# Sparse attention and an MLP on one core: the weights' differences taken earlier and spread, the first two half-size products in PSUM tiles of their own, sums moved, the last store on another queue

## The chip, the cores and the metric

The kernel runs on one core of one Trainium2 chip. The core has a matrix engine (TensorE, PE in the profile; PEld is its weight load), a vector engine (VectorE, DVE), an activation engine (ScalarE, ACT), GpSimd (POOL), and SyncE (SP), which here issues DMAs alone. Each engine takes its own instructions strictly in order; semaphores tie the engines together. The metric is the device time of one execution in microseconds (us).

## The reference, cut to what matters

```python
# 4 batches, 8 heads, 768 tokens, head size 64: block-sparse attention
scores = where(mask, q @ k.T / 8, -1e9);  attn = softmax(scores)      # 24 blocks of 32 tokens
x = concat over heads of (attn @ v)                                   # 4 x 768 x 512
# then a residual MLP with affine scales
a1 = alpha1 * x + beta1
u  = x + lam * (w_tok @ a1)                # mixes the 768 tokens
a2 = alpha2 * u + beta2
out = u + lam * (relu(a2 @ w_ch1) @ w_ch2) # 512 -> 2048 -> 512
```

The mask allows a band, the first and last block, and three drawn blocks for each block of rows.

## The kernel before

The 768 tokens of a batch lie in 6 tiles of 128 partitions. Attention goes by pairs of heads, 16 in all (4 batches of 4 pairs). For one pair: scores on PE (L600) into PSUM tiles named `sp` (2 buffers of two banks) or `mm`; the exponential on ACT (L618) into `eT`; for all but the first five pairs a multiplication by a 0/1 mask on DVE (L635); the product with v on PE (L670) into the one-bank tile `op`, which has a single buffer; and on DVE the division by the row sums (L687, L688), which writes `x_sb` and sets `op` free. POOL (in a few places DVE) then makes `a1pp` from it (L704, L705). Token mixing is L844 on PE, its sum L856 on DVE, a cast `ubf` (L863), a transposition by DMA (`uraw`, L894, issued by SP) or by PE (L872), and the second affine to `uT` (L885 on DVE, L883 on ACT for the last batch). The first MLP layer is L910 on PE with a Relu on ACT (L917) into `hts`. The second layer is L930 with its sum on DVE (L939), or, for some tiles of the last two batches, the scheme below. A store of a finished tile is issued by SP (L943).

The scheme: a token tile t and the tile t+3 are taken together, and their second layer is computed with 7 half-size products in place of 8 (Winograd's form of Strassen's method). The operands are four quarters of `hts` (11, 12 for tile t; 21, 22 for tile t+3; the second digit is the half of the 2048 hidden units) and four quarters of `w2b`, the weights already scaled by lam. Needed beside them are

- the **differences** of weights, T1 to T4, 16 instructions of 128 x 512 elements in bf16 on DVE (L972), made once; they are put where the transposed q and k of the first five pairs were (`qTs`, `kTs`), and into `qk` and `tmore`;
- the **sums** S1 to S4 of hidden values for each t, 128 x 1024 in bf16 on DVE (L1018): S1 = 21 + 22, S2 = S1 - 11, S3 = 11 - 21, S4 = 12 - S2;
- the seven products (L1044), each 8 matmuls of 128 x 256, and the adds of their results to `x_sb` (L1054).

Batch 2 uses it for t = 1 and 2, batch 3 for t = 0, 1, 2. In batch 2, **product 1** of a pair goes into an `mm` tile (3 one-bank buffers, shared with the scores, both MLP layers and the token mixing). DVE adds it to the second half of tile t (128 x 256) and to both halves of tile t+3 (128 x 512). **Product 2** then accumulates onto the same bank, and the total is added to the first half of tile t (128 x 256). Since it writes to what the first two adds read, it waits for them.

The order of all work is written out by hand. After the first five pairs, the rows of `WEAVE` (`W1` 9 rows, `W2` 12, `W2L` 12, `W3` 4) list letters, and each letter emits one job on all its engines: `q` scores of three units, `x` an exponential, `k` a mask multiplication, `p` a product with v, `f` a group of the first layer, `g` the next piece of the second layer or the next product, `T` a token-mixing job, `A` the next difference, `S` the next sum of hidden values, and so on. So a letter's place in a row sets the place of its instruction in each engine's queue. `W2` runs while the pairs of batch 2 are in attention (from about 105 us on), `W2L` while those of batch 3 are (to about 234 us), and `W3` does the rest. In `W2L`, 16 `A`s stand in the first nine rows: the differences run from 172.7 to 224.9 us. Two stretches of the profile are of the same make and are spoken of below as **stretch A** (120.5 to 133 us, in batch 2) and **stretch B** (189 to 203 us, in batch 3): in both, DVE does a division, masks, two `uT` affines, masks, a division, one L939 sum, masks and a division almost without a pause.

Of the kernel before, what the change touches and what calls it, by code (L numbers as in the profile page):

```python
# [20 lines left out]
S = 768  # L21
# [21 lines left out]
W1 = [  # L43
# [9 lines left out]
]  # L53
W2 = [
# [12 lines left out]
]  # L67
W2L = [
# [12 lines left out]
]  # L81
W3 = [
# [5 lines left out]
STR = (2, 3)  # L88
HN = NH // 2
HC = DM // 2  # L90
WEAVE = W1 + W2 + W2L + W3
ENG = {
    "kT0": 0,
    "kT1": 0,
# [153 lines left out]
def kernel(  # L248
# [16 lines left out]
    nc = tc.nc  # L265
# [194 lines left out]
    def sp_tile():  # L460
        return psum.tile([P, 2, 512], FP, name="sp", tag="sp", bufs=2)
# [6 lines left out]
    def mm_tile(shape=(P, DM), dt=FP):  # L468
        return psum.tile(list(shape), dt, name="mm", tag="mm", bufs=3)

    def op_tile(shape):
        phase["op"] += 1
        if phase["first"] and phase["op"] % 2 == 0:
            return mm_tile(shape)
        return psum.tile(shape, FP, name="op", tag="op", bufs=1)
# [463 lines left out]
            nc.vector.tensor_tensor(out=x, in0=x, in1=ps[:], op=ALU.add)  # L939
            emit_store(b, o, slice(0, DM))  # L940

    def emit_store(b, o, sl):
        nc.sync.dma_start(  # L943
            out[b].rearrange("(p o) n -> p o n", o=NT)[:, o, sl], x_sbs[b][:, o, sl]
        )

# [12 lines left out]
    def b_rows(name, n, k=1):  # L959
        if name in bq:  # L960
            rows, cols = bq[name]
            return w2b[:, rows.start + n : rows.start + n + k, cols]
        m = HN * ("T1", "T2", "T4", "T3").index(name) + n
        assert m // 6 == (m + k - 1) // 6
        return tpool[m // 6][:, m % 6 : m % 6 + k]
# [3 lines left out]
    def job_t(dst, a, b, n, k=2):  # L969
        for name in (a, b):  # L970
            assert name in bq or (name, n) in did
        nc.vector.tensor_tensor(  # L972
            out=b_rows(dst, n, k),
            in0=b_rows(a, n, k),
            in1=b_rows(b, n, k),
            op=ALU.subtract,
        )
        did.add((dst, n))
# [10 lines left out]
    def a_of(b, t, name, r=slice(0, HN)):  # L989
        if name in ("X1", "X2"):  # L990
            return xs[(b, t, name)][:, r]
        c, half = {"11": (0, 0), "12": (0, 1), "21": (1, 0), "22": (1, 1)}[name]
        return hts[(b, c)][:, HN * half + r.start : HN * half + r.stop, ts(t, P)]
# [40 lines left out]
    def mul(b, t, n, ps, start, cols=slice(0, HC)):  # L1034
        a, m, need = PROD[n]
        assert m in bq or all((m, r) in did for r in range(0, HN, 2))
        if need:
            assert all(("S", b, t, need, r) in did for r in range(HN))
        c, half = {"1": (0, 0), "X": (1, 0)}.get(a[0], (1, 0))
        if need == 0:  # L1040
            h, half = divmod(int(a) - 11, 10)
            assert all(("f", b, h, HN * half + r) in did for r in range(HN))
        for r in range(HN):
            nc.tensor.matmul(  # L1044
                ps,
                a_of(b, t, a)[:, r],
                b_rows(m, r)[:, 0, cols],
                start=(start and r == 0),
                stop=(r == HN - 1),
                skip_group_check=True,  # L1050
            )

    def plus(x, ps):
        nc.vector.tensor_tensor(out=x, in0=x, in1=ps, op=ALU.add)  # L1054

    def twice(ps):
        return ps.unsqueeze(1).broadcast_to([P, 2, HC])

    lo, hi = slice(0, HC), slice(HC, DM)

    def job_p(b, t, n):
        x = x_sbs[b]
        tail = b == B - 1
        last = tail and t == NT // 2 - 1
        if n == 1 or (n == 6 and not tail):
            if n == 1 and not tail:
                banks[(b, t)] = [mm_tile()[:]]
            else:
                banks[(b, t)] = [sp_tile()[:, 0]]
        bk = banks[(b, t)]  # L1070
        if n == 7:
            bk.append(mm_tile()[:])
        elif n == (2 if tail else 3):
            bk.insert(1, mm_tile()[:])
        if n == 1:
            mul(b, t, 1, bk[0][:, lo], True)
            if tail:
                plus(x[:, t, lo], bk[0][:, lo])
            else:
                plus(x[:, t, hi], bk[0][:, lo])  # L1080
                plus(
                    x[:, t + 3].rearrange("p (h c) -> p h c", h=2), twice(bk[0][:, lo])
                )
        elif n == 2:
            ps = bk[1] if tail else bk[0]
            mul(b, t, 2, ps[:, lo], tail)
            if last or not tail:
                plus(x[:, t, lo], ps[:, lo])
            if last:
                emit_store(b, t, lo)  # L1090
        elif n == 6:
            mul(b, t, 6, bk[0][:, lo], not tail)
            plus(x[:, t + 3, lo], bk[0][:, lo])
        elif n == 7:
            mul(b, t, 7, bk[-1][:, lo], True)
            plus(x[:, t + 3, hi], bk[-1][:, lo])
        elif n == 5:
            mul(b, t, 5, bk[0][:, lo], False)
            plus(x[:, t : t + 4 : 3, hi], twice(bk[0][:, lo]))
        elif n == 4:  # L1100
            mul(b, t, 4, bk[-1][:, lo], False)
            plus(x[:, t + 3, lo], bk[-1][:, lo])
            emit_store(b, t + 3, slice(0, DM))
        elif last:
            for h in range(2):
                sl = slice(HC + h * P, HC + h * P + P)
                ps = (mm_tile(), op_tile([P, DM]))[h]
                mul(b, t, 3, ps[:, sl], True, ts(h, P))
                plus(x[:, t, sl], ps[:, sl])
                emit_store(b, t, sl)  # L1110
        else:
            mul(b, t, 3, bk[1][:, hi], not tail)
            sl = slice(0, DM) if tail else hi
            plus(x[:, t, sl], bk[1][:, sl])
            emit_store(b, t, slice(0, DM))
        did.add((b, t, n))
# [36 lines left out]
    def start_mlp(b):  # L1153
        ns = [n // 2 + HN * (n % 2) for n in range(NH)] if b == B - 1 else range(NH)
        todo["f"] += [lambda c=c, n=n: job_f1(b, c, n) for c in range(2) for n in ns]
        if b not in STR:
            todo["g"] += [
                lambda o=o, g=g: job_f2(b, o, g) for o in range(NT) for g in range(4)
            ]
            return  # L1160
        todo["g"] += [
            lambda j=j: job_p(b, *j) if len(j) == 2 else job_f2(b, *j[:2])
            for j in P_ORDER[b]
        ]
        todo["S"] += [lambda t=t, n=n, r=r: job_s(b, t, n, r) for t, n, r in S_ORDER[b]]
# [206 lines left out]
    todo["A"] = [lambda t=t, n=n: job_t(*t, n) for t in T_ORDER for n in range(0, HN, 2)]  # L1372
    for p, text in enumerate(WEAVE):
        for t in text.replace(" ", ""):
# [30 lines left out]
```

## Time and profile before

| | |
|---|---|
| median of 3 runs | 303.78 us (303.64 to 304.06) |
| profiled execution | 305.7 us, span of its instructions 304.0 us |
| busy in the span | PE 292.7, DVE 220.4, ACT 218.8, POOL 111.5 us |
| granted TensorE clock | 1.00 throughout |

The profile is of one execution. Starts are counted from the first instruction. In the timeline a row gives start, length, engine, line, operation, out<-in with shapes and xcount for successive instructions of one kind; a bracket gives the idle time of that engine before it and what ended it. Matmuls overlap each other in the records: a group of 8 with 128 x 256 is recorded 1.03 to 1.05 us long, and the next group starts 0.87 us after it began.

### The profile page before, as it was taken

Reading aid. Unit: us, or ns where it says so; the run is one execution under the profiler, and the core shown is the slowest. Engines: PE = TensorE matmul, PEld = TensorE weight load, DVE = VectorE, ACT = ScalarE, POOL = GpSimd, SP = SyncE. Lnnn points to the kernel's source line nnn. Section 1 sums busy time; section 2 is a strip of 40 time slices with the busy share of each in tenths; the row PEclk is TensorE's granted clock in tenths of the full one; section 3 lists DMA queues with packets and bytes.
Section 4 is the critical chain, followed back from the end, with each engine's and each line's share of the span. In section 5 each row is a group of like instructions: output and inputs, shape, how many; then the busy total and the mean of one; then the engine's idle time right before and its main releaser. Section 6 shows DMA issues by size and latency. Waiting matters only on the chain.

```text
span 304.0 us, 7518 instructions
## 1 busy us (share of the span) xinstructions
PE 292.7 (96%) x3113; PEld 194.1 (64%) x3113; DVE 220.4 (72%) x434; ACT 218.8 (72%) x324; POOL 111.5 (37%) x151
## 2 busy tenths in 40 slices
PE   7899999999999999999999999899998889999995
PEld 2678778665577565555675565455565667766885
DVE  4978889995688797963568897993877778204574
ACT  5999989998899954998888754898769524577100
POOL 8997877632534700564315410353322020000000
PEclk9999999999999999999999999999999999999999
DMA  6999999971491992729737592828112002200032
GB/s 178 203 195 164 189 150 198 174 124 26 94 156 40 141 188 67 133 43 152 121 56 92 104 179 75 120 64 130 44 23 54 2 32 57 112 0 2 0 115 95
DMA packets 57275, 31.09 MB, mean 102 GB/s; under 512 B 37205, under 2 KB 54017, under 8 KB 57241
## 3 DMA queue, kind: packets, MB, share of 16 engines
q0 software_dynamic: 16752, 14.22, 32.8%
q1 hardware_dynamic: 40164, 15.99, 27.3%
q8 instruction: 24, 0.39, 0.5%
q10 hardware_dynamic: 324, 0.40, 0.5%
q14 instruction: 11, 0.08, 0.1%
HBM read 29.75 MB, written 6.29 MB: 119 GB/s over the span
## 4 chain that ended last, share of the span: by engine, by line
PE 79%; DVE 9%; DMA 6%; ACT 2%; POOL 2%; issue 1%; SPq 0%; POOLq 0%
PE mm L910 25%; PE mm L930 14%; PE sp L600 8%; PE mm L844 7%; PE op L670 7%; PE mm L1044 5%; PE sp L1044 3%; DMA qpad<-in_q_dram 3%; PE mm L600 3%; DVE eT L635 2%; DMA uraw<-ubf 2%; ACT eT L618 2%; PE op L647 2%; PE mm L820 1%; DVE x_sb L1054 1%
## 5 line engine op out<-in xcount | busy, mean ns | idle before, releaser
L618 ACT ACTIVATE eT<-sp,expb 128x1024 f16<-128x1024 f32 x111 | 118.4, 1119 | 3.5 <-PE sp L600 2.9
L910 PE MATMUL mm<-uT,w1b 128*128 128x384 bf16 x512 | 91.6, 326 | 0.0
L635 DVE TENSOR_TENSOR eT<-eT,mask 128x1024 f16<-128x1024 f16 x99 | 80.8, 843 | 12.8 <-ACT eT L618 12.6
L704 POOL TENSOR_TENSOR a1pp<-x_sb,vbc 128x384 bf16<-128x384 f32 x26 | 28.7, 1105 | 131.8 <-DVE x_sb L688 96.9
L917 ACT ACTIVATE hts<-mm 128x384 bf16<-128x384 f32 x128 | 61.0, 500 | 19.3 <-PE mm L910 18.6
L910 PEld LDWEIGHTS <-w1b 128*128 128x128 bf16 x512 | 48.1, 98 | 31.8 <-issue 2.1
L618 ACT ACTIVATE eT<-mm,expb 128x512 f16<-128x512 f32 x66 | 41.7, 685 | 27.5 <-PE mm L600 27.2
L930 PE MATMUL mm<-w2b,hts 128*128 128x512 bf16 x224 | 54.7, 379 | 0.0
L670 PEld LDWEIGHTS <-eT 128*128 128x128 f16 x792 | 29.8, 98 | 10.9 <-DVE x_sb L688 2.3
L670 PE MATMUL op<-vext,eT 128*128 128x65 f16 x792 | 32.3, 194 | 1.8 <-DVE x_sb L688 0.8
L930 PEld LDWEIGHTS <-hts 128*128 128x128 bf16 x224 | 19.7, 97 | 22.4 <-issue 3.9
L705 POOL TENSOR_TENSOR a1pp<-a1pp,vbc 128x384 bf16<-128x384 bf16 x26 | 27.8, 1068 | 2.1
L600 PE MATMUL sp<-qTs,kTs 88*128 88x512 bf16 (+1 forms) x120 | 26.9, 325 | 0.9 <-DVE kTs L488 0.6
L844 PE MATMUL mm<-a1pp,wtokT 128*128 128x256 bf16 x216 | 25.9, 273 | 0.0
L844 PEld LDWEIGHTS <-wtokT 128*128 128x128 bf16 x216 | 20.7, 98 | 5.3 <-issue 1.8
L1044 PEld LDWEIGHTS <-hts 128*128 128x128 bf16 x208 | 19.5, 98 | 6.3 <-issue 2.9
L856 DVE TENSOR_TENSOR x_sb<-x_sb,mm 128x512 f32<-128x512 f32 x18 | 12.3, 685 | 11.0 <-PE mm L844 11.0
L600 PE MATMUL sp<-qhT,khT 64*128 64x256 bf16 (+1 forms) x176 | 19.8, 322 | 0.0
L600 PEld LDWEIGHTS <-khT 64*128 64x128 bf16 x264 | 10.5, 94 | 12.5 <-issue 9.0
L647 PEld LDWEIGHTS <-eT 128*128 128x128 f16 x360 | 14.9, 97 | 3.8 <-issue 0.3
L1018 DVE TENSOR_TENSOR xs<-hts 128x512 bf16<-128x512 bf16 (+1 forms) x8 | 3.7, 486 | 17.8 <-ACT hts L917 17.8
L688 DVE TENSOR_TENSOR x_sb<-op,rcp 128x384 f32<-128x384 f32 x28 | 15.6, 557 | 1.0
(117 smaller groups left out, 322.9 us busy)
## 6 DMA issues: line engine op xcount, KB each, us to landing
out_dram<-x_sb SPq DMA_DIRECT2D x23, 256.0 KB
qpad<-in_q_dram POOLq DMA_DIRECT2D x15, 192.0 KB, 4.2
kr<-in_k_dram POOLq DMA_DIRECT2D x15, 192.0 KB, 5.6
vr<-in_v_dram POOLq DMA_DIRECT2D x15, 192.0 KB, 6.2
w1b<-in_moe_w_ch_dram POOLq DMA_DIRECT2D x4, 512.0 KB, 10.0
w2b<-in_moe_w_ch_dram POOLq DMA_DIRECT2D x4, 512.0 KB, 8.7
hts<-in_moe_w_tok_dram POOLq DMA_DIRECT2D x2, 576.0 KB, 9.1
x_sb<-in_k_dram ACTq DMA_DIRECT2D x2, 192.0 KB
```

Of the source, the lines that this page charges most:

```text
L600: nc.tensor.matmul(sp[jj][:, dst], lhsT, rhs, start=True, stop=True, skip_group_check=True,)
L618: nc.scalar.activation(dst, at, AF.Exp, bias=expb[:], scale=SCALE)
L635: nc.vector.tensor_mul(out=e, in0=e, in1=keep)
L647: nc.tensor.matmul(op[0][:, o, :], ets[u][:, jj, h * QB + n * P : h * QB + n * P + P], vexts[i % NVB][:, w, 2 * jp + jj, :], start=op[1] == 0,
L670: nc.tensor.matmul(op[0][:, o, :], ets[u][:, jj, h * QB + n * P : h * QB + n * P + P], vexts[i % NVB][:, w, 2 * jp + jj, :], start=op[1] == 0,
L704: eng.tensor_tensor(out=dst, in0=x_sbs[b][:, :, cols], in1=bc[0], op=ALU.mult)
L705: eng.tensor_tensor(out=dst, in0=dst, in1=bc[1], op=ALU.add)
L844: nc.tensor.matmul(ps[:, o], wtokT[:, os_, ts(2 * n + o, P)], a1pps[i][:, os_, :], start=(os_ == 0 and o == 0), stop=(os_ == NT - 1 and o ...
L910: nc.tensor.matmul(ps[:, 0:QC], w1b[:, dk, ts(n, P)], uTs[b][:, dk, ts(c, QC)], start=(dk == 0), stop=(dk == 3),)
L917: nc.scalar.activation(hts[(b, c)][:, n, :], ps[:, 0:QC], AF.Relu)
L930: nc.tensor.matmul(ps[:], ht[:, nk, ts(o % 3, P)], w2b[:, nk, :], start=(nk == 0), stop=(nk == NH - 1),)
L1044: nc.tensor.matmul(ps, a_of(b, t, a)[:, r], b_rows(m, r)[:, 0, cols], start=(start and r == 0), stop=(r == HN - 1), skip_group_check=True,)
```

## The change

1. The rows of `W2` are replaced by `W2A`, which has one `A` in each of its 12 rows; `W2L` keeps four (rows 6 to 9). In the instruction order of DVE the 16 differences so begin 64 us earlier: the first stands behind the `a1pp` of DVE at 108 us (before: the first at 172.7 us), the third to sixth stand in stretch A, and stretch B holds none before its last division.
2. In batch 2, product 1 is added by one instruction to all four quarters of tiles t and t+3 (128 x 2 x 512 elements; the product is read with zero strides), and product 2 gets an `mm` tile of its own and is added to the first half of tile t by itself.
3. The sums are moved. For t = 1, S1 and S2 now stand ahead of the joined add of t = 2, and S4, with S1 of t = 2, ahead of the last division. S2, S3 and S4 of t = 2 stand between and behind the three sums of the last token mixing, L856 (before, all behind them).
4. The last of the two 128-column stores at the end is issued by ScalarE's queue in place of SP's.

The order of PE's instructions is the same in both kernels, and so are the order on POOL, and that on ACT but for the store.

```diff
-WEAVE = W1 + W2 + W2L + W3
+WEAVE = W1 + W2A + W2L + W3
@@ W2A, from W2: one A in each row; three of the rows @@
-    "q 0 p k x v Q v 1 2 p k x g k g",
+    "q 0 p k x v Q v 1 2 p A k x g k g",
-    "q 0 p 1 g x k f K k x f p p k 2 f",
+    "q 0 p 1 g x A k f K k x f p p k 2 f",
-    "q k 0 f x f p s f f x 1 L p k 2 f f f k Y f",
+    "q A k 0 f x f p s f f x 1 L p k 2 f f f k Y f",
...
@@ W2L, its last two rows @@
-    "q x 0 x K k g d k s f g f 1 k p p g 2",
-    "q Y x x S S S k g k 0 1 k 2 p g v g v g",
+    "q x 0 x K k g d k s f g f 1 k p p S S g 2",
+    "q Y S x k g k 0 1 k 2 p g v g v g",
@@ W3, its first row @@
-    "p p p g s g g T T T S S S d g g U g v S S g g g g g f f f f",
+    "p p S S p g s g g T S T S T S d g g U g v g g g g g f f f f",
...
-    def emit_store(b, o, sl):
-        nc.sync.dma_start(
+    def emit_store(b, o, sl, eng=nc.sync):
+        eng.dma_start(
...
         if n == 1:
             mul(b, t, 1, bk[0][:, lo], True)
             if tail:
                 plus(x[:, t, lo], bk[0][:, lo])
             else:
-                plus(x[:, t, hi], bk[0][:, lo])
+                both = x[:, t : t + 4 : 3].rearrange("p o (h c) -> p o h c", h=2)
                 plus(
-                    x[:, t + 3].rearrange("p (h c) -> p h c", h=2), twice(bk[0][:, lo])
+                    both, bk[0][:, lo].unsqueeze(1).unsqueeze(1).broadcast_to(both.shape)
                 )
         elif n == 2:
-            ps = bk[1] if tail else bk[0]
-            mul(b, t, 2, ps[:, lo], tail)
+            ps = bk[1] if tail else mm_tile()
+            mul(b, t, 2, ps[:, lo], True)
...
-                emit_store(b, t, sl)
+                emit_store(b, t, sl, (nc.sync, nc.scalar)[h])
```

More of the change, by code (lines that the diff above doesn't have):

```diff
@@ L67 @@
 ]
-W2L = [
[9 rows of a table removed]
+W2A = [
[12 rows of a table added]
+]
+W2L = [
[9 rows of a table added]
     "q x 0 x T k 1 k f 2 k f Q f d p L",
[2 rows of a table removed]
[2 rows of a table added]
 ]
 W3 = [
[1 row of a table removed]
[1 row of a table added]
     "f f f f f f f f f f f f",
```

28 rows, old and new, of tables (W2A, W2L) are left out of this document.

## The prediction

> **What bounds the kernel now.** I read the page's busy times first, then the waits of PE, then windows, then the timeline of the places found.
>
> ```profile
> PE 292.7 (96%) x3113; PEld 194.1 (64%) x3113; DVE 220.4 (72%) x434; ACT 218.8 (72%) x324; POOL 111.5 (37%) x151
> ```
> ```profile
> PE mm L1044 <- DVE x_sb L1054: 1.9, 2, 1.6
> ...
> PE op L670 <- DVE x_sb L688: 0.8, 1, 0.8
> PE op L670 <- DVE eT L635: 0.8, 1, 0.8
> PE mm L1044 <- DVE hts L1018: 0.7, 1, 0.7
> ```
> ```profile
> 120.00:140.00 20.00, 20.00 (x206) 11.51 (x203) 14.80 (x23) 18.40 (x31) 11.38 (x12) 1.00 0.58 96
> 190.00:200.00 10.00, 9.14 (x109) 4.85 (x105) 9.56 (x16) 8.43 (x13) 4.25 (x4) 1.00 0.77 125
> 200.00:210.00 10.00, 9.86 (x83) 5.74 (x82) 7.22 (x13) 9.09 (x19) 4.50 (x5) 1.00 0.41 57
> ```
>
> PE is busy for 96% of the span, so time can only come out of PE's pauses. The waits (total, times, longest) show the four that this change can touch: 1.9 us before a second product, 0.8 on a division, 0.8 on a mask, 0.7 on a sum, 4.2 us together. The windows (length, then busy time of each engine) say where PE is without a pause: in 120 to 140, which holds stretch A, it has none. Stretch B lacks 0.86 and 0.14 us. So a delay of DVE in stretch A is a new loss, and one taken out of stretch B is a gain of 1.0 us at most, and a little more, since a matmul's record reaches about 0.17 us past its share of the pipe (a group of 8 is recorded 1.03 us long and the next starts 0.87 us after it began).
>
> **Part 1, the products' own tiles and the moved sums.** Its stage:
>
> ```profile
> 233.70 1.00 POOL L704 TENSOR_TENSOR a1pp<-x_sb,vbc 128x384 bf16<-128x384 f32 x1 [10.47 <-DVE x_sb L688]
> ...
> 233.83 1.41 DVE L635 TENSOR_TENSOR eT<-eT,mask 128x1024 f16<-128x1024 f16 x1 [0.22 <-ACT eT L618]
> ...
> 235.17 1.00 DVE L1054 TENSOR_TENSOR x_sb<-x_sb,mm 128x256 f32<-128x256 f32 x2
> ...
> 236.22 1.03 PE L1044 MATMUL mm<-w2b,hts 128*128 128x256 bf16 x8 [1.58 <-DVE x_sb L1054]
> ...
> 237.09 0.81 PE L910 MATMUL mm<-uT,w1b 128*128 128x384 bf16 x4
> ...
> 239.55 1.02 DVE L1054 TENSOR_TENSOR x_sb<-x_sb,mm 128x256 f32<-128x256 f32 x2 [1.24 <-PE mm L1044]
> ...
> 239.87 1.27 ACT L618 ACTIVATE eT<-mm,expb 128x512 f16<-128x512 f32 x2 [1.44 <-PE mm L600]
> ...
> 240.62 1.03 PE L1044 MATMUL mm<-w2b,hts 128*128 128x256 bf16 x8 [0.35 <-DVE x_sb L1054]
> ...
> 243.35 1.29 DVE L635 TENSOR_TENSOR eT<-eT,mask 128x1024 f16<-128x1024 f16 x2
> ...
> 244.78 0.56 DVE L688 TENSOR_TENSOR x_sb<-op,rcp 128x384 f32<-128x384 f32 x1
> ...
> 245.39 1.28 PE L670 MATMUL op<-vext,eT 128*128 128x65 f16 x36 [0.78 <-DVE x_sb L688]
> 245.41 1.00 POOL L704 TENSOR_TENSOR a1pp<-x_sb,vbc 128x384 bf16<-128x384 f32 x1 [9.39 <-DVE x_sb L688]
> ...
> 246.71 0.20 DVE L687 RECIPROCAL rcp<-op 128x6 f32<-128x6 f32 x1 [1.37 <-PE op L670]
> ...
> 248.12 0.56 DVE L705 TENSOR_TENSOR a1pp<-a1pp,vbc 128x384 bf16<-128x384 bf16 x1
> ...
> 249.12 4.09 PE L844 MATMUL mm<-a1pp,wtokT 128*128 128x256 bf16 x36
> ...
> 253.25 0.69 DVE L856 TENSOR_TENSOR x_sb<-x_sb,mm 128x512 f32<-128x512 f32 x1 [0.62 <-PE mm L844]
> ...
> 257.78 0.83 PE L1044 MATMUL mm<-qk,hts 128*128 128x256 bf16 x6 [0.74 <-DVE hts L1018]
> ...
> 258.64 1.03 ACT L883 ACTIVATE uT<-uraw,ab2T 128x768 bf16<-128x768 bf16 x1 [2.32 <-DMA uraw<-ubf]
> ...
> 261.33 2.93 PE L910 MATMUL mm<-uT,w1b 128*128 128x384 bf16 x17
> ```
> ```profile
> L1054 DVE TENSOR_TENSOR x_sb<-x_sb,mm x22: 288/421/689, 235.2 to 300.3; 128x256 f32<-128x256 f32 x17, 128x512 f32<-128x512 f32 x4, 128x128 f32<-128x128 f32 x1
> ```
>
> The last row gives shortest, median and longest: 288 ns for 128 columns, 421 for 256, 689 for 512, that is 0.13 us and 1.05 ns a column. A joined add of 1024 isn't in the trace. Bounds: 0.69 us, as if the second half cost nothing, and 4 x 0.42 = 1.68 us. I take the slope: 0.13 + 1024 x 1.05 ns = 1.2 us, since it fits three sizes. It replaces 1.00 us for the pair at 235.17.
>
> I walk along PE, with all times on before's scale.
> - Product 2 of t = 1: PE stood free from 236.22 - 1.58 = 234.64. It has its own bank now and starts there. But the first-layer group behind it (237.09) takes product 1's bank, and waits for the joined add: the mask at 233.83 lets go at 235.17, so 235.17 + 1.2 = 236.4. The wait isn't removed, it moves one group on. Gain 237.09 - 236.44 = 0.65.
> - Product 2 of t = 2 (240.62): its bank is that of the scores just before, freed by the exponential at 239.87, of which the first of two ends at 240.5. Moved by 0.65 this is 239.9; gain 0.7, so the wait of 0.35 stays almost whole.
> - The division at 244.78 ends at 245.34 and lets PE go on at 245.39; PE had been free 0.78 earlier, at 244.61, with the gain of 0.7 at 243.9. DVE from 236.3 on: mask 0.6, add 0.35, mask 0.6, S1 0.6, S2 0.7, joined add 1.2, S3 0.6, mask 0.6, add 0.35, two masks 1.2 (1.29 for a pair in the row at 243.35), division 0.8; sum 7.6, which ends at about 244.0 (the sums fill the 1.24 us for which DVE waited for product 1 of t = 2 at 239.55). So PE goes on at 244.05 and is held by DVE, not by PE. Gain 1.3.
> - Token mixing (249.12) needs POOL's `a1pp` and the one of DVE (248.12 + 0.56 = 248.68, so 0.44 to spare). Now S4 and an S1 stand before the last division. S4 starts with POOL's multiply (245.41 before, just behind the division), and S1 runs beside it. The mask at 233.83, which ran beside POOL's at 233.70, took 1.41 in place of 0.69. With 0.65 + 1.4 DVE is 2.05 later at a place where it used to sit idle for 1.37 (246.71): 0.65 late, 0.44 of it spare. Loss 0.2.
> - Product 7 of t = 2 (257.78) waited 0.74 for S3, 0.9 with the overhang. S2 and S3 now stand in the pauses in which DVE waited for PE between the sums L856 (0.62 at 253.25, for a sum of 0.6 to 0.7), S4 just behind: all three are done some 3 us before that product. Gain 0.9.
>
> Sum 1.3 - 0.2 + 0.9 = 2.0. Is the cover gone? The first layer of batch 3 (261.33) needs the `uT` that ACT ends at 259.67; its DMA moves with the token mixing (1.1 earlier), the first layer by 2.0, so 0.7 of the 1.6 stays. Behind it PE has no pause up to the last product, and the 2.0 reach the end. Bounds for this part: 0.9 (both joined adds at 1.68: PE goes on 0.9 later at the division) and 2.3 (add at 0.69, no loss to POOL).
>
> In the Trainium skill, SBUF — State Buffer, section Who interferes with whom, a DVE instruction with both inputs in SBUF is blocked by a GpSimd one that reads SBUF only until that one ends. By it S1 would start when POOL's multiply of 1.00 us ends and be through 0.3 us sooner, the token mixing would not be late, and this part would be 2.2. The mask at 233.83 agrees (POOL's multiply ends at 234.70, the mask 0.5 later); no row here shows S1 in that place.
>
> **Part 2, the differences.** They cost 0.42 us each (median), 0.34 where DVE goes on without a pause:
>
> ```profile
> L972 DVE TENSOR_TENSOR qTs<-w2b x4: 417/420/1140, 172.7 to 181.5; 128x512 bf16<-128x512 bf16 x4
> ```
> ```profile
> 121.20 3.42 DVE L635 TENSOR_TENSOR eT<-eT,mask 128x1024 f16<-128x1024 f16 x3
> ...
> 121.44 1.31 POOL L704 TENSOR_TENSOR a1pp<-x_sb,vbc 128x384 bf16<-128x384 f32 x1 [15.21 <-PE mm L600]
> ...
> 121.78 0.91 PE L670 MATMUL op<-vext,eT 128*128 128x65 f16 x24
> ```
> ```profile
> 190.08 2.81 DVE L635 TENSOR_TENSOR eT<-eT,mask 128x1024 f16<-128x1024 f16 x2
> ...
> 190.32 0.54 PE L670 MATMUL op<-vext,eT 128*128 128x65 f16 x12
> ...
> 191.62 0.54 PE L670 MATMUL op<-vext,eT 128*128 128x65 f16 x12 [0.75 <-DVE eT L635]
> ...
> 194.62 0.48 DVE L885 TENSOR_SCALAR uT<-uraw,ab2T 128x768 bf16<-128x768 bf16 x1 [0.41 <-DMA uraw<-ubf]
> ...
> 196.78 0.56 DVE L688 TENSOR_TENSOR x_sb<-op,rcp 128x384 f32<-128x384 f32 x1
> ...
> 197.39 0.91 PE L670 MATMUL op<-vext,eT 128*128 128x65 f16 x24
> ```
>
> Stretch A, before: the first mask starts at 121.20, ahead of POOL's multiply at 121.44, and PE's 24 products with v from 121.78 run through. In stretch B a difference stands first, so POOL's multiply comes ahead of the mask: two masks take 2.81, the first of them until PE's next products at 191.62, 1.5, and PE's 24 fall apart into 12 at 190.32 and 12 at that time. The second 12 were due at 190.32 + 0.37 = 190.69, so 0.93 are lost. With the third difference between the division and the mask stretch A becomes what stretch B was: **loss 0.9**. Behind it PE is 0.9 later, and the three other differences of stretch A (0.34 each, 1.14 at the longest) come to no more than that; I take none for them.
>
> Stretch B loses its five differences, and its first mask is ahead of POOL as it was in A: 0.93 come back. But DVE then meets the `uT` affine at 194.62, which waits for the DMA of `uraw`, and in SP's order that DMA stands behind a store of a tile whose sum (L939) waits for PE, not for a difference. So DVE is held until 194.62 again, and from there only one difference goes: the division ends at 196.78 + 0.56 - 0.34 = 197.0. PE, due at 197.39 less its pause (10.00 - 9.14 - 0.75 = 0.11), 0.17 of overhang and 0.93, that is 196.2, waits 0.85. Of the 1.0 of pauses and 3 x 0.17 of overhang, 1.5 in all, 0.9 stays: **gain 0.6**. Bounds 0.2 (DMA 0.4 later) and 1.5 (DMA no bound). The other ten differences land outside both stretches, and those that go leave 172 to 189; none of PE's waits above lies at either place: 0, at most 0.2 on either side.
>
> **Part 3, the last store.**
>
> ```profile
> 300.79 0.29 DVE L1054 TENSOR_TENSOR x_sb<-x_sb,op 128x128 f32<-128x128 f32 x1 [0.16 <-PE op L1044]
> ```
> ```profile
> 301.24 0.41 SPq L943 DMA_DIRECT2D out_dram<-x_sb  x1
> ```
>
> The last add ends at 301.08 and SP sends the store at 301.24, 0.16 later, so SP wasn't late. Another queue saves at most these 0.16; its first use since the start of the kernel could cost as much as the 0.41 of an issue. I take 0.
>
> **Sum.** 304.0 - 2.0 + 0.9 - 0.6 = 302.3 for the span. The profiled execution took 305.7, 1.7 more than its span and 1.9 more than the median of 303.78. The same 1.7 off the median: 302.1 us.
>
> **The rivals.**
> - *The DMA is no bound in stretch B.* In stretch A the two affines ran without a wait, so `uraw` can come sooner. Then the gain there is 1.5: 303.78 - 2.6 = 301.2. Chance 0.20.
> - *The joined add costs 1.68.* Reading one bank four times over may run as four adds. Part 1 is then 0.9: 303.2. Against it: the 512-column adds, of which some read a product twice, take the same 0.69. Chance 0.10.
> - *Nothing comes of it.* The wait moves from product 2 to the next group whole, since DVE's work in that stage is not less, and only product 7's gain pays for stretch A: 303.78 within 0.2%. For it: the division at 244.78 follows DVE's work. Against: DVE was idle for 1.24 and 1.37 us there. Chance 0.05.
> - *Slower.* The four differences of stretch A are each held up by POOL's multiply and add, and all come through to PE: 4 x 1.14, the longest of the row, in place of 0.9, which makes 303.78 - 2.0 + 4.6 - 0.6 = 305.8. It decides from a loss of 2.6 in stretch A, 0.65 for each. Against: the median of 0.42, and PE's dues, which move with the first delay. Chance 0.13. The Trainium skill, SBUF — State Buffer, Who interferes with whom, speaks for it: whichever of the two starts second is blocked.
>
> **How the numbers follow.** The forecast, 302.1 (301.5 to 302.9 by its bounds), has 0.52. With 0.20 for the first rival and 0.10 for the second it fills 300.9 to 303.4, where the low end takes the DMA's gain with part 1's upper bound in part. 0.2% is 0.6 us, about what a measurement here can tell from no change: faster 0.82, same 0.05, slower 0.13.
>
> **What would show it.** Right: no pause before product 2 of t = 1 and one of about 1 us before the first-layer group behind it; the pause before product 2 of t = 2 still there, with an exponential behind it; none before product 7 of t = 2; joined adds of 1.2 us; one pause of 0.75 us in stretch A on a mask, and in stretch B one on the division in place of three. Wrong: several pauses in stretch A, a joined add over 1.5 us, a pause ahead of the first layer of batch 3, or an end more than 0.3 us longer after the last add.

## The result, and the profile after

The kernel after takes 302.37 us (median of 5 executions, 302.20 to 302.73) where the kernel before, beside it, took 303.78 (303.64 to 304.37): a ratio of 0.995, 95% interval 0.9936 to 0.9965. It is faster, by 1.4 us; the forecast was 302.1 us. A later comparison gave 302.27 against 303.82 us, the same ratio (0.9937 to 0.9964).

The profiled execution of after took 302.2 us with a span of 300.1. The spans of the two profiles so differ by 3.9 us, the medians by 1.4. That gap is what the experiments had to explain first.

PE's waits after the change (what waits, what for: total, times, longest):

```profile
PE mm L924 <- DVE x_sb L1068: 0.9, 1, 0.9
...
PE op L684 <- DVE eT L649: 0.8, 1, 0.8
...
PE mm L1058 <- ACT eT L632: 0.3, 1, 0.3
```

Lines lie 14 lower here than in before (L1044 is L1058, L910 is L924). Before, four waits of 4.2 us stood in this list. Now the second product waits for no add; the first-layer group (L924) waits 0.9 for the joined add in its place. One wait on a mask is there, as before, but it is another one, in stretch A.

The stage of the products in the timeline of after:

```profile
232.24 1.41 DVE L649 TENSOR_TENSOR eT<-eT,mask 128x1024 f16<-128x1024 f16 x1 [0.22 <-ACT eT L632]
...
232.88 1.04 PE L1058 MATMUL mm<-w2b,hts 128*128 128x256 bf16 x8
...
233.19 1.25 POOL L719 TENSOR_TENSOR a1pp<-a1pp,vbc 128x384 bf16<-128x384 bf16 x1
233.58 1.21 DVE L1068 TENSOR_TENSOR x_sb<-x_sb,mm 128x1024 f32<-128x1024 f32 x1
...
234.84 0.81 PE L924 MATMUL mm<-uT,w1b 128*128 128x384 bf16 x4 [0.92 <-DVE x_sb L1068]
...
237.57 1.21 DVE L1068 TENSOR_TENSOR x_sb<-x_sb,mm 128x1024 f32<-128x1024 f32 x1
...
238.36 1.03 PE L1058 MATMUL mm<-w2b,hts 128*128 128x256 bf16 x8 [0.34 <-ACT eT L632]
...
242.23 0.68 DVE L1032 TENSOR_TENSOR hts<-hts,xs 128x1024 bf16<-128x1024 bf16 x1
242.37 1.27 PE L684 MATMUL op<-vext,eT 128*128 128x65 f16 x36
242.39 1.38 POOL L718 TENSOR_TENSOR a1pp<-x_sb,vbc 128x384 bf16<-128x384 f32 x1 [7.96 <-DVE x_sb L702]
242.83 1.49 DVE L1032 TENSOR_TENSOR xs<-hts 128x1024 bf16<-128x1024 bf16 x1
...
246.26 4.11 PE L858 MATMUL mm<-a1pp,wtokT 128*128 128x256 bf16 x36
...
254.03 0.82 PE L1058 MATMUL mm<-qk,hts 128*128 128x256 bf16 x6
```

Product 2 of t = 1 (232.88) starts without a pause. The joined add takes 1.21 us, and the group behind it pauses 0.92. Product 2 of t = 2 keeps its 0.34, on an exponential. The division's pause and that ahead of product 7 (254.03) are gone. S1 (242.83), beside POOL's multiply, takes 1.49 us in place of 0.68.

Stretch A of after:

```profile
120.20 0.41 DVE L986 TENSOR_TENSOR qTs<-w2b 128x512 bf16<-128x512 bf16 x1
...
120.44 1.04 POOL L718 TENSOR_TENSOR a1pp<-x_sb,vbc 128x384 bf16<-128x384 f32 x1 [15.21 <-PE mm L614]
...
120.53 3.42 DVE L649 TENSOR_TENSOR eT<-eT,mask 128x1024 f16<-128x1024 f16 x3
120.78 0.54 PE L684 MATMUL op<-vext,eT 128*128 128x65 f16 x12
...
122.08 0.54 PE L684 MATMUL op<-vext,eT 128*128 128x65 f16 x12 [0.76 <-DVE eT L649]
```

The difference lets POOL's multiply (120.44) in ahead of the first mask (120.53), and PE's 24 products with v fall apart into 12 and 12 with a pause of 0.76. That is what stretch B looked like before. In stretch B of after the 24 run through at 190.26:

```profile
189.10 0.33 SPq L957 DMA_DIRECT2D out_dram<-x_sb  x1
...
189.48 2.26 SPq L908 DMA_TRANSPOSE uraw<-ubf  x1
...
190.26 0.91 PE L684 MATMUL op<-vext,eT 128*128 128x65 f16 x24
...
193.03 1.09 DVE L899 TENSOR_SCALAR uT<-uraw,ab2T 128x768 bf16<-128x768 bf16 x2
...
196.13 0.90 PE L684 MATMUL op<-vext,eT 128*128 128x65 f16 x24
```

**A ledger by sections.** PE's order is the same in all these kernels, so a time can be taken between the same two PE groups in each profile. I cut the span at starts of groups in the timeline, named here by their start in before: the scores at 41.74 us, the products with v at 119.70, the second layer at 146.72 and 188.61, the first layer at 206.75, the scores at 232.11, the products with v at 237.74 and 245.39, the token mixing at 249.12, a product at 258.71. *Head* is from the span's start to the first cut, *A* from 119.70 to 146.72 (27.0 us), *B* from 188.61 to 206.75, *group* (with the first-layer group) to 237.74 from 232.11, *division* to 245.39, *mixing* to 249.12, *product 7* to 258.71. The remaining sections, 41.74 to 119.70, 146.72 to 188.61, 206.75 to 232.11 and 258.71 to the last add, repeat within 0.03 us in all profiles. *Outside* is the device time less the span, over all executions of the kernel.

| kernel | head | A | B | group | division | mixing | product 7 | span | outside | median us |
|---|---|---|---|---|---|---|---|---|---|---|
| before, first profile | 41.74 | 27.03 | 18.14 | 5.63 | 7.65 | 3.72 | 9.59 | 304.0 | 1.7 | 303.78 |
| before, again (e1) | 40.44 | 27.02 | 18.00 | 5.63 | 7.65 | 3.72 | 9.60 | 302.5 | 1.7 to 1.8 | 303.71 |
| after, first profile | 40.74 | 27.96 | 16.61 | 4.96 | 6.89 | 3.89 | 8.64 | 300.1 | 2.0 to 2.1 | 302.37 |
| after, again (e5) | 41.35 | 27.96 | 16.97 | 4.96 | 6.88 | 3.89 | 8.64 | 301.1 | 2.0 to 2.1 | 302.27 |
| differences only (e2) | 40.20 | 27.97 | 16.61 | 5.63 | 7.65 | 3.72 | 9.59 | 301.8 | 1.7 | 304.01 |
| products and sums only (e3) | 40.17 | 27.03 | 17.66 | 4.96 | 6.89 | 3.89 | 8.64 | 299.7 | 1.7 | 301.45 |
| products only (e10) | 40.23 | 27.03 | 17.66 | 4.96 | 7.86 | 3.72 | 9.59 | 301.5 | 1.7 to 1.8 | 303.32 |
| last store only (e12) | 40.18 | 27.03 | 17.66 | 5.63 | 7.65 | 3.72 | 9.59 | 301.9 | 2.0 to 2.1 | 304.13 |
| third difference behind mask (e4) | 40.17 | 27.73 | 17.22 | 4.96 | 6.89 | 3.89 | 8.64 | 299.9 | 2.0 to 2.1 | 301.62 |
| differences in gaps (e7) | 40.32 | 27.03 | 17.32 | 4.97 | 6.88 | 3.89 | 8.64 | 299.5 | 2.0 to 2.1 | 301.33 |
| second transposition early (e8) | 40.36 | 27.96 | 16.61 | 4.97 | 6.88 | 3.89 | 8.64 | 299.7 | 1.8 to 1.9 | 301.52 |
| last store on SP (e6) | 39.90 | 27.96 | 16.61 | 4.97 | 6.88 | 3.89 | 8.64 | 299.3 | 1.7 | 301.88 |
| own tile, two adds (e9) | 40.11 | 27.96 | 17.00 | 4.76 | 6.89 | 3.88 | 8.64 | 299.7 | 2.0 to 2.1 | 301.82 |
| joined improvements (e11) | 40.16 | 27.03 | 16.61 | 4.76 | 6.88 | 3.72 | 8.63 | 298.3 | 1.7 to 1.8 | 300.01 |

Two columns move without an edit: the head (39.9 to 41.7), which holds the waits for the first loads, and B. All others take the same value to 0.02 us wherever the same edit is in. The kernels of e9 and e11 leave out an add (see e9), and their 4.76 is not comparable with the 4.96.

A profile shows one execution, but the span is on record for nearly all. Since every section but the head and B repeats, an execution's span less those sections gives its *head and B* together. The medians of this, in us: 58.0 in 72 executions of before, 57.5 in the ten of after (first profile and e5), 57.3 in the 42 of the seven kernels that have no difference in B ahead of its last division and issue the DMA of `uraw` behind a store (these ten among them), and 56.9 in the ten of e8 and e11, which issue it earlier. Single executions spread over 0.4 to 2 us around these.

### The profile page after: what moved, and what is told of

Same layout as the page of the kernel before. It is cut to its first block, busy times and chain, and to the rows that moved or that the text cites. A ratio compares the mean times of both kernels' runs of the same rounds, so it can differ in the third digit from the quotient of the medians.

```text
span 300.1 us, 7518 instructions
## 1 busy us (share of the span) xinstructions
PE 292.3 (97%) x3113; PEld 194.3 (65%) x3113; DVE 220.1 (73%) x432; ACT 218.6 (73%) x324; POOL 112.2 (37%) x151
## 4 chain that ended last, share of the span: by engine, by line
PE 92%; DVE 3%; ACT 2%; DMA 1%; issue 1%; POOL 0%; POOLq 0%
PE mm L924 27%; PE mm L944 16%; PE sp L614 11%; PE op L684 8%; PE mm L858 8%; PE mm L1058 6%; PE sp L1058 4%; PE mm L614 3%; PE mm L834 3%; PE op L661 2%; ACT eT L632 2%; PE mm L661 1%; DMA x_sb<-in_q_dram 1%; DVE eT L649 1%; PE mm L524 1%; PE mm L812 1%
## 5 line engine op out<-in xcount | busy, mean ns | idle before, releaser
L924 PE MATMUL mm<-uT,w1b 128*128 128x384 bf16 x512 | 91.6, 326 | 0.9 <-DVE x_sb L1068 0.9
L924 PEld LDWEIGHTS <-w1b 128*128 128x128 bf16 x512 | 48.1, 98 | 32.9 <-issue 3.2
L632 ACT ACTIVATE eT<-mm,expb 128x512 f16<-128x512 f32 x66 | 41.7, 685 | 27.5 <-PE mm L614 27.2
L1058 PEld LDWEIGHTS <-hts 128*128 128x128 bf16 x208 | 19.6, 98 | 3.5 <-issue 1.1
L1032 DVE TENSOR_TENSOR xs<-hts 128x512 bf16<-128x512 bf16 (+1 forms) x8 | 4.5, 587 | 17.8 <-ACT hts L931 17.8
```

Of the source, the lines that this page charges most:

```text
L632: nc.scalar.activation(dst, at, AF.Exp, bias=expb[:], scale=SCALE)
L924: nc.tensor.matmul(ps[:, 0:QC], w1b[:, dk, ts(n, P)], uTs[b][:, dk, ts(c, QC)], start=(dk == 0), stop=(dk == 3),)
L1058: nc.tensor.matmul(ps, a_of(b, t, a)[:, r], b_rows(m, r)[:, 0, cols], start=(start and r == 0), stop=(r == HN - 1), skip_group_check=True,)
```

## The experiments

**e1, the kernel before once more.** No edit.

> The kernel before, unchanged, profiled once more. The two traces differ by 3.9 us in their spans (304.0 and 300.1), the medians by only 1.4. Theory A: the first profile of before was an unlucky execution; its waits for loads at 38 and 41 us (0.65 and 0.19 us) and the late DMA of `uraw` in stretch B (pauses of 0.75, 0.11 and 0.14 us) are partly gone in this one, and its span is 301.5 to 302.5 us. Theory B: these waits belong to the kernel, the span is again 303.5 to 304.5 and the time outside the span differs instead. Both: the pauses of 1.59, 0.35, 0.78 and 0.75 us around the products of batch 2 are here again.

303.71 us (303.44 to 304.28), span 302.5. The waits for loads at 38 and 41 us are gone: the first profile of before was an unlucky execution, by 1.3 us in the head. So 3.9 was not the size of the change. B is nearly as long as in the first profile (18.00 for 18.14), though the wait for the DMA of `uraw` fell from 0.41 to 0.27 us. The time outside the span is nearly the same in all executions of before (1.66 to 1.78).

**e2, the differences alone** (before, with `W2A` and the four `A`s of `W2L`).

```diff
-WEAVE = W1 + W2 + W2L + W3
+WEAVE = W1 + W2A + W2L + W3
```

> The kernel before with the differences' new places alone. By the two traces: a pause of about 0.76 us on a mask comes into stretch A (0.92 us of PE's time with the overhang) and the three pauses of stretch B go (1.5 us): 303.78 + 0.92 - 1.5 = 303.2 us. By the prediction (gain of 0.6 in B): 304.1 us. Rival: in a usual execution stretch B loses only the pause of 0.75 us on the mask, since the DMA is not late there; then what comes in A is what goes in B, and the time is 303.8, the same as before.

304.01 us, ratio 1.0008 (0.9998 to 1.0018): no gain that can be told from nothing, rather a loss. In its profile A loses 0.95 and B gains 1.39 against e1; but B alone can differ by 0.7 between executions, and this profiled one, 303.52, was the fastest of its kernel. By the medians, what comes in A is about what goes in B (head and B together: 57.3 us here, 58.0 in before).

**e3, the products and the sums alone** (before, with items 2 and 3 of the change).

```diff
-            ps = bk[1] if tail else bk[0]
+            ps = bk[1] if tail else mm_tile()
...
-    "q Y x x S S S k g k 0 1 k 2 p g v g v g",
+    "q Y x S x k g k 0 1 k 2 p g v g v g",
```

(The row with the third `S` is given as the kernel has it; in the diff of the section on the change its first `x` was left out by mistake.)

> The kernel before with product 2's own tile, the joined add and the sums' new places, the differences where before has them. By the two traces this part is worth 0.67 at the first-layer group, 0.77 more at the division, -0.16 at the token mixing and 0.89 at product 7: 2.17 us, so 301.6 us (the prediction's 2.0: 301.8). Rival: part of it is lost behind the token mixing or to the differences' stalls in batch 3, and it is worth no more than 1.4: 302.4 us.

301.45 us, ratio 0.9926 (0.9913 to 0.9938). The four sections give 0.67, 0.76, -0.17 and 0.95: 2.21. This part is the whole gain; the change as a whole is 0.8 to 0.9 us slower than it.

**e12, the last store alone.**

```diff
-                emit_store(b, t, sl)
+                emit_store(b, t, sl, (nc.sync, nc.scalar)[h])
```

> The kernel before with the last store on ScalarE's queue and nothing else. By the time outside the span (1.66 to 1.78 us in every execution of kernels whose last store SP issues, 1.8 to 2.1 us where ScalarE does) and a stretch after the last add that is 0.05 us shorter: 303.78 + 0.3 = 304.1 us, slower. By the prediction, which put nothing on this part: 303.8 us. The three parts alone would then stand at +0.2 (differences), -2.35 (products and sums) and +0.3 us (store), together -1.85, against -1.5 for the change as a whole.

304.13 against 303.88 us beside it, ratio 1.0009 (1.0000 to 1.0018). The profile's tail (start, length, queue):

```profile
298.32 0.81 SPq L943 DMA_DIRECT2D out_dram<-x_sb  x2
298.76 0.29 DVE L1054 TENSOR_TENSOR x_sb<-x_sb,op 128x128 f32<-128x128 f32 x1 [0.16 <-PE op L1044]
299.08 0.35 ACTq L943 DMA_DIRECT2D out_dram<-x_sb  x1
```

The store is issued 0.03 us after the last add ends, in place of 0.16, and the span's stretch after that add is 0.05 shorter (2.85 for 2.90). Yet the time outside the span is 2.00 to 2.08 in place of 1.67 to 1.78 in the executions of before beside it. The trace doesn't show what runs there; that it hangs on ScalarE's queue the next experiment confirms.

**e6, after with the last store on SP again.**

```diff
-                emit_store(b, t, sl, (nc.sync, nc.scalar)[h])
+                emit_store(b, t, sl, nc.sync)
```

> The kernel after with the last store back on SP's queue. The prediction put nothing on this part. In the profiles the time outside the span is 1.7 us with SP's store (1.7, 1.72, 1.7) and 2.05 us with ScalarE's (2.1, 2.06), while the stretch from the last add to the span's end is 2.86 to 2.90 us with the one and 2.82 to 2.85 us with the other. Theory: the second queue costs 0.3 us outside the span, so this kernel takes 302.1 us. Rival: the difference outside the span is chance, and it takes 302.4 us.

301.88 us (301.01 to 302.87) against 302.27 (301.9 to 303.1) of e5 beside it. The time outside is 1.67 to 1.76 in all its executions, so 0.33 of the difference is shown there.

**e5, after once more.** No edit.

> The kernel after, unchanged, for a second profile and as the measure of the three runs beside it. In stretch B the second `uT` affine waited 0.80 us for its DMA in the run with the third difference moved (PE paused 0.44 us on the division behind it), 0.14 us in the first profile of after (no pause), and nothing in the run of the differences alone. Theory: that DMA lands 4.0 to 5.1 us after its issue by chance, so the executions of after spread over 0.6 us; this profile shows a wait between 0 and 0.8 us, and the median is 302.2 to 302.5 us. Time outside the span 2.05 us, as in the first profile of after.

302.27 us, and B is 16.97: a pause of 0.19 us on the division, with the overhang 0.36 more than in the first profile. The head took 41.35, with a wait of 0.93 for a load of q at 40.67 us. Both profiles of after have longer heads (40.74, 41.35) than those of the other changed kernels (39.90 to 40.36), where nothing of the change lies.

**e4, the third difference behind the mask.**

```diff
-    "q g 0 k g d 1 2 p x A k g x k",
+    "q g 0 k g d 1 2 p x k A g x k",
```

> The kernel after with one letter moved: the third difference, which stands between the division and the first mask of stretch A, comes behind that mask. Theory: the mask then starts ahead of POOL's multiply, runs 0.68 us, and the pause of 0.76 us before PE's second dozen of products with v at 122 us is gone: 302.37 - 0.9 = 301.5 us. Rival: POOL's multiply only meets the next mask instead, DVE loses the same 1.5 us, and the pause appears at the next wait of PE for DVE (the division at 126 us): 302.2 to 302.4 us.

301.62 us, but stretch A is only 0.23 shorter than in after (27.73). Its timeline:

```profile
119.63 0.68 DVE L649 TENSOR_TENSOR eT<-eT,mask 128x1024 f16<-128x1024 f16 x1
...
119.87 1.30 POOL L718 TENSOR_TENSOR a1pp<-x_sb,vbc 128x384 bf16<-128x384 f32 x1 [15.20 <-PE mm L614]
...
120.21 0.91 PE L684 MATMUL op<-vext,eT 128*128 128x65 f16 x24
120.23 1.23 DVE L986 TENSOR_TENSOR qTs<-w2b 128x512 bf16<-128x512 bf16 x1
...
126.46 0.91 PE L684 MATMUL op<-vext,eT 128*128 128x65 f16 x24 [0.21 <-DVE x_sb L702]
```

The pause on the mask is gone, as the theory had it. But now the difference itself meets POOL's multiply and takes 1.23 us in place of 0.41, and DVE's lag comes out at the next two divisions (0.21 here and 0.14 behind it, 0.70 with the overhang). So the rival was right in the main: what stands next in DVE's queue pays for POOL, and the lag of the differences travels to the next wait. That the median fell by 0.65 to 0.75 isn't explained by this section. The rest lies in head and B, whose median is 57.1 us in the five executions here against 57.5 in after; nothing was edited there, so it is scatter as far as is known. In the profiled execution B was even 0.6 longer than in the first profile of after, with the DMA late:

```profile
188.29 0.34 SPq L957 DMA_DIRECT2D out_dram<-x_sb  x1
...
188.68 2.92 SPq L908 DMA_TRANSPOSE uraw<-ubf  x1
...
193.48 0.48 DVE L899 TENSOR_SCALAR uT<-uraw,ab2T 128x768 bf16<-128x768 bf16 x1 [0.80 <-DMA uraw<-ubf]
...
195.92 0.91 PE L684 MATMUL op<-vext,eT 128*128 128x65 f16 x24 [0.44 <-DVE x_sb L702]
```

**e7, the differences in DVE's gaps** (all other `A`s of both blocks taken out; this row in both).

```diff
-    "q A k 0 f x f p s f f x 1 L p k 2 f f f k Y f",
+    "q k 0 f x f p s f f x 1 L p k 2 f f f k A A A A A A A A Y f",
```

> The kernel after with all 16 differences taken out of their places and put, eight at a time, ahead of two copies of v for which DVE stands idle 3.3 us and 3.4 us (140.1 and 209.8 us in the run of the products and sums alone). None stands in stretch A or B. Theory: the section of stretch A goes back from 28.27 to 27.34 us, B stays at 17.2 to 17.8, and the time is 302.37 - 0.93 = 301.4 us. Rival: the differences cost where they go, since PE runs without a pause there and eight of them (2.7 us) delay the copy of v or a mask behind it: 302.4 us or more.

301.33 us (300.73 to 301.95), 0.94 less than e5 beside it, and A is back at 27.03:

```profile
134.04 1.42 DVE L986 TENSOR_TENSOR qTs<-w2b 128x512 bf16<-128x512 bf16 x4
...
140.90 0.37 DVE L342 COPY vext<-vr 128x768 f16<-128x768 f16 x1 [2.98 <-DMA vr<-in_v_dram]
...
193.03 0.48 DVE L899 TENSOR_SCALAR uT<-uraw,ab2T 128x768 bf16<-128x768 bf16 x1 [0.89 <-DMA uraw<-ubf]
...
195.47 0.91 PE L684 MATMUL op<-vext,eT 128*128 128x65 f16 x24 [0.54 <-DVE x_sb L702]
```

The first eight differences run from 134.04 on in one piece, and DVE still waits 2.98 us for v behind them: they are free where DVE waits. B was 17.32 in this profile, with a wait of 0.89 us for the DMA and no difference near it: so the pause on the division in B is the DMA's alone.

**e8, the second transposition ahead of the store.**

```diff
-    "q g 0 k g d 1 2 p x k g x k",
+    "q d g 0 k g 1 2 p x k g x k",
```

(in `W2L`)

> The kernel after with the second transposing DMA of stretch B issued ahead of the 256 KB store that stood before it on SP's queue; the order on the other engines is the same. Theory: that DMA is what holds the second affine, so its wait is gone, no division in stretch B waits, and the median falls by the usual loss of the executions that were late, 0.2 to 0.5 us, to 301.9 to 302.2 us, with a narrower spread. Rival: what is late is not the queue but the transposition itself beside other traffic; the wait stays as it was and the time is 302.4 us.

301.52 us (301.12 to 303.13), 0.75 less than e5. The DMA goes out ahead of the store, some 3 us sooner, and B is 16.61:

```profile
184.73 2.54 SPq L908 DMA_TRANSPOSE uraw<-ubf  x2
188.72 0.34 SPq L957 DMA_DIRECT2D out_dram<-x_sb  x1
...
192.64 0.86 DVE L899 TENSOR_SCALAR uT<-uraw,ab2T 128x768 bf16<-128x768 bf16 x2
194.84 0.56 DVE L702 TENSOR_TENSOR x_sb<-op,rcp 128x384 f32<-128x384 f32 x1
```

The two affines run in 0.86 us without a wait. Of the 0.75 us, 0.55 lie in head and B (56.9 for 57.5 by the medians) and 0.2 outside the span. Two things here are not explained: the spread is no narrower, and the time outside the span is 1.81 to 1.87, though ScalarE still issues the last store.

**e10, the products alone** (e3 without its moved sums).

> The kernel before with product 2's own tile and the joined add alone; the sums and the differences stay where before has them. Theory: DVE sets the division's time, and without sums to do it stands idle about 1 us ahead of product 1 of t = 2, with three sums (2.0 us) behind it, so 0.67 us are gained at the first-layer group but the division comes 0.9 us later than in after and gives nothing or takes a little back; product 7 keeps its pause of 0.75 us. In all a gain of 0.5 us: 303.3 us. Rival: the own tile carries the division as well (0.67 + 0.76) and the moved sums only give product 7: 302.4 us.

303.32 us, ratio 0.9986 (0.9976 to 0.9996), as the theory had it. The pauses of its timeline:

```profile
234.43 0.81 PE L910 MATMUL mm<-uT,w1b 128*128 128x384 bf16 x4 [0.92 <-DVE x_sb L1054]
...
236.90 1.22 DVE L1054 TENSOR_TENSOR x_sb<-x_sb,mm 128x1024 f32<-128x1024 f32 x1 [0.98 <-PE mm L1044]
...
242.94 1.28 PE L670 MATMUL op<-vext,eT 128*128 128x65 f16 x36 [0.99 <-DVE x_sb L688]
```

DVE stands idle 0.98 us ahead of the second joined add, with the sums behind it, and the division makes PE wait 0.99. The own tile with the joined add gives 0.67 at the group and loses 0.21 of it at the division. The moved sums give the rest: 1.75 of the 2.21.

**e9, own tile and two adds** (after, with the two adds of before in place of the joined one).

```diff
-                both = x[:, t : t + 4 : 3].rearrange("p o (h c) -> p o h c", h=2)
-                plus(
-                    both, bk[0][:, lo].unsqueeze(1).unsqueeze(1).broadcast_to(both.shape)
-                )
+                plus(x[:, t, hi], bk[0][:, lo])
+                plus(
+                    x[:, t + 3].rearrange("p (h c) -> p h c", h=2), twice(bk[0][:, lo])
+                )
```

> The kernel after with product 2's own tile kept, but product 1 added by the two instructions of before in place of the joined one. The joined add took 1.21 us in all profiles of after, the pair 1.00 us from the start of the first to the end of the second. Theory (DVE's queue sets this stage, and the joined add is no saving): the pause ahead of the first-layer group shrinks from 0.92 to 0.72 us, the division comes a little earlier too, and the stage is 0.2 us shorter, 302.1 us. Rival: the tile alone isn't enough, the joined add spares DVE an instruction that matters, and the stage is as long or longer: 302.3 us or more.

301.82 us (301.69 to 302.16), beside a before of 303.74: ratio 0.9938 (0.9924 to 0.9953). But this kernel leaves work out. In before, the first half of tile t got products 1 and 2 together, since product 2 accumulated onto product 1's bank. With a tile of its own product 2 comes there alone, and the two adds bring product 1 to the other three quarters only, 768 of the 1024 columns. So in e9, and in e11, the first halves of tiles 1 and 2 of batch 2 lack product 1.

```profile
233.33 1.00 DVE L1068 TENSOR_TENSOR x_sb<-x_sb,mm 128x256 f32<-128x256 f32 x2
...
234.39 0.81 PE L924 MATMUL mm<-uT,w1b 128*128 128x384 bf16 x4 [0.72 <-DVE x_sb L1068]
```

The pause shrinks from 0.92 to 0.72 and the section from 4.96 to 4.76; the division's section stays. These 0.2 us are what the fourth quarter costs, not what joining costs. Separate adds for all four quarters would take a third one of 256 columns: 0.41 us, begun 0.07 before the end of the one ahead as these are, so 1.00 + 0.34 = 1.34 us against the 1.21 of the joined add. That is an estimate from these rows; no run shows it.

**e11, the improvements joined**: e7, e8, e6, e9, and S1 of t = 2 moved from before the last division to behind two more pieces of the second layer (`"p p S p g s g g S T S T S T S d ..."`).

> The kernel after with the changes that the runs so far speak for: all differences in DVE's two long gaps, the second transposing DMA of stretch B ahead of the store, the last store on SP's queue, two adds in place of the joined one, and the sum S1 of t = 2 moved from before the last division to behind the next products. If the gains add up: 0.93 in stretch A, 0.3 in stretch B (its section always 16.6 us), 0.33 outside the span, 0.2 at the joined adds and 0.17 at the token mixing, 1.9 us in all: 300.4 us. Rival: the sum S1 and the early transposition cost elsewhere what they give (a copy to `ubf` later, a queue of transpositions): 300.9 us or more.

300.01 us (299.97 to 300.39), ratio to before 0.9881 (0.9865 to 0.9897): faster than both kernels, by 3.7 and 2.3 us, but with the add of one quarter left out as in e9. With the joined add, whose section is 0.20 longer in all profiles, 300.2 us is to be expected; that is an estimate and was not run. Every section has the shortest value of the table (27.03, 16.61, 4.76, 6.88, 3.72, 8.63), so the gains add up. The mixing section, 3.88 or 3.89 wherever S1 of t = 2 stands before the last division, is back at 3.72. Of PE's waits that touch the change two remain:

```profile
PE mm L924 <- DVE x_sb L1068: 0.7, 1, 0.7
...
PE mm L1058 <- ACT eT L632: 0.3, 1, 0.3
```

## Why the prediction was right, point by point

- **Joined add**: taken as 1.2 us by the slope, measured 1.21. Right.
- **The wait moves to the first-layer group**: forecast gain 0.65, measured 0.67, with a pause of 0.92 (said: about 1). Right.
- **Product 2 of t = 2** keeps its pause on an exponential (0.35 forecast, 0.34 measured). Right.
- **The division**: gain forecast as 1.3 in all, 0.67 + 0.76 = 1.43 measured. The prediction counted 7.6 us of DVE work up to there and so found that PE is held by DVE. PE's pause is now 0.03, so the two arrive together; e10 shows DVE's side when the sums stand elsewhere.
- **Token mixing** 0.2 late: measured 0.17. **Product 7**: gain 0.9 forecast, 0.95 measured. Part 1 in all: 2.0 forecast, 2.21 by the sections.
- **S1 beside POOL.** S1 took 1.49 us and ended 0.55 after POOL's multiply (242.39 + 1.38 = 243.77, 242.83 + 1.49 = 244.32), and the mixing was late, as the rows of before had said. By the Trainium skill, SBUF — State Buffer, section Who interferes with whom, the engine that issues second waits for the other's whole instruction. The trace agrees, on both sides: POOL's multiply, started while S4 ran, took 1.38 in place of 1.00, and S1 then waited for it. The prediction read the rule with a multiply of 1.00 us and so came to no loss; the rule was right and the length put into it was not. The same section of the Trainium skill says that a DVE instruction with at most one input in SBUF, outside its 2-port modes, doesn't contend. The trace agrees: the joined add, whose other input is PSUM, took 1.21 beside POOL's add (233.19) and 1.21 without it (237.57).
- **Stretch A**: loss 0.9 forecast, 0.93 measured, at the mask, by POOL's multiply. Right. The rival in which four differences each come through at 1.14 us is excluded: nothing is added behind the first.
- **Stretch B**: gain 0.6 forecast, 0.5 to 0.7 measured, in part by luck. The step was "0.9 of 1.5 stays", because DVE is held by the DMA of `uraw`. The mechanism is there: in the profiles without differences in B the division waits 0, 0.19, 0.21, 0.44 or 0.54 us, and e8 takes the wait away by an earlier DMA. But when the DMA lands differs from execution to execution. In single profiles B loses 0 (e2, e6 and the first profile of after) to 0.71 (e7), and with the differences 1.05 (e3, e10 and e12) to 1.53 (the first profile of before), so pairs of profiles give a gain anywhere from 0.3 to 1.5 us. The head's order is the same in all kernels, so the medians of head and B are the better measure: 58.0 before, 57.5 in after and 57.3 in the 42 executions. Against the 56.9 of e8 and e11, whose B lost nothing in either profile, B usually loses 1.1 us with the differences and 0.5 to 0.6 without. So both numbers of the step were 0.3 to 0.4 too large, since the first profile of before was a late execution, and the two errors cancelled.
- **The last store**: forecast 0, measured a loss of 0.25 by the medians of e12, 0.33 by the time outside the span. The prediction looked for the price inside the span ("at most these 0.16") and bounded it by an issue of 0.41; it didn't look at the time outside at all. This step was wrong.
- **The sum.** The change is worth +0.93 in A, -0.5 in head and B by the medians, -2.21 in the four sections of part 1, -0.05 in the tail and +0.33 outside: -1.5 us, where the medians of the whole change say -1.4 and -1.55. The parts alone, e2 (+0.2), e3 (-2.35) and e12 (+0.25), make -1.9; with intervals of 0.3 to 0.4 us on each of them, a loss that only the whole change has is not shown. Nor is a longer wait for the first loads: the heads of the two profiles of after (40.74, 41.35) are long, but e6, whose order is the same up to the last store, had the shortest (39.90), and its executions have a head and B of 57.4 against 57.5. The forecast of -1.7 was near by its mechanisms and also by errors that cancel: part 1 was 0.2 too small, and the store, with the tail, 0.3 too good.

## What to carry to other kernels

Where the order of one engine is the same in two kernels, compare the profiles section by section between the same groups of that engine, and profile the old kernel twice: a single span here carried 1.3 us of luck in the loads. Before a section's change is put down to an edit, see by the spans of all executions how much it moves by itself. An instruction that is moved was free here where its engine waits for data (e7); put ahead of a mask in a busy stretch, one of 0.41 us let POOL start ahead of DVE and cost 0.93. Where a shared result is split in two, see that each part still gets both: e9 and e11 gained 0.2 us by an add that they lack. Count an end-of-kernel change against the device time, not against the span.

## What was not expected

- The last store on ScalarE's queue makes the device time 0.3 us longer outside the recorded span (2.0 to 2.1 us, against 1.65 to 1.78 in every execution in which SP issues it), though the store itself goes out 0.13 us sooner. In e8 it was 1.81 to 1.87.
- A transposing DMA issued behind a store of 256 KB on the same queue let the affine that needs it go 4.9 us after its issue in e7 (188.12 to 193.03), 4.8 in e4, 5.1 in the first profile of before, and at most 4.0 in e2, with the same order on SP's queue in all four. Issued ahead of the store, it was not late in either profile (e8, e11).
- One add over four quarters took 1.21 us; the pair over three quarters took 1.00 from the first's start to the second's end, in which DVE began the second 0.07 us before the first ended (e9). By the column the joined add is no slower.
